# Turning M5's result back on VectorE instead of TensorE in the last unit of a fused attention and expert kernel

## The chip, the cores and the metric

The kernel runs on one core of one Trainium2 chip. A core has five engines that run beside each other, each with an instruction queue of its own: TensorE (PE, with PEld for its weight loads), VectorE (DVE), ScalarE (ACT), GpSimd (POOL) and SyncE (SP), which here does nothing but issue transfers. Transfers between the core's memory and HBM are issued from SP's queue and, now and then, from ScalarE's; the core's 16 DMA engines move the data. The metric is the device time of one execution in microseconds, lower being better.

## The reference

A block-wise attention with decay gives `x`, 3072 tokens by 512. Four experts follow, each two products with a ReLU between, and their results are summed with a weight per token:

```
def _moe_ref(x, domain_probs, w1, w2):
    p = domain_probs / (domain_probs.sum(-1, keepdims=True) + 1e-09)
    out = np.zeros((N, D), dtype=np.float32)
    for e in range(E):                      # E = 4, D = 512, F = 1024
        h = np.maximum(x @ w1[e], 0.0)
        out += p[:, e:e + 1] * (h @ w2[e])
    return out
```

Everything is float32. The change touches only the way in which one part of `out`, for the last 1024 tokens, is written.

## The kernel before, in words

The tokens are worked in three groups of 1024; a unit is one group with one expert, twelve units in all. Each expert product is a Strassen-like product of seven parts, M1 to M7, over 2 x 2 blocks, so that TensorE does seven block products instead of eight. In the later units the second product is nested: each of the seven is again made of seven inner ones (`nested_product`; `inner` issues one of them, with the matmuls of line 1550 and the VectorE adds into `sums`, recorded at line 117). `SEQ3`, line 1271, is the order of the outer products in a nested unit: M1, M3, M5, M7, M6, M2, M4. `INNER`, line 328, is the order of the inner ones: M1, M7, M6, M4, M5, M2, M3. Two banks of TensorE's output memory take turns in an outer product; `READ` says which inner product goes on in a bank that VectorE has read before.

`sums[m]` holds the result of outer product m for all the experts of the last group, features on the partitions and tokens along the free axis: four pieces of 128 x 256, piece 2*dd + t for feature half dd and token half t. After the last unit's products the seven are added into each other (`to_join`, `joined`, `bring`, `add`), and M2, M3, M4 and M5 then hold the four quadrants of `out` (`RESULT`). M5's quadrant is token half 1 and feature half 1. Since `out` has tokens along its rows, each quadrant has to be turned. Two helpers do that:

- `give(m, t, tags, dds)` (line 1369): 128 x 128 transposes by TensorE into a bank (line 1377; four of them for both feature halves), one ScalarE copy of the bank to a tile `y` (line 1381), and one transfer of 256 rows with 1 KB each, issued by SP (`send`, line 114).
- `give_across(m, dd, t)` (line 1390): one VectorE transpose in blocks of 32 x 32 (line 1398, 128 x 256), and four transfers (line 1402) of 256 pieces of 128 bytes each, 32 KB in all; the second of the four is issued by ScalarE, the other three by SP.

The last outer product, M4, is taken to its end on TensorE: `turn_end` (line 1440) turns its first feature half into a bank and `turned_product` (line 1450) adds the last two inner products there; ScalarE copies (line 1454) and SP stores. M4's other feature half goes through `give` with one `dd`.

The engines' queues hold their instructions in the order in which the program issues them, and an engine does not pass a waiting instruction. The order in the last unit is written out by hand. For outer product i the list `order` has eight slots; slot x holds some of the inner products. After slot x > 0 the loop takes the next entry of `after_last[SEQ3[i]]` and turns what it names. With M2 as the outer product these are M3's pieces, by `give_across`; with M4, before the change, M5's two token halves after slots 1 and 2 and M2's two after slots 3 and 4, by `give`. For M4, slots 1, 3, 5 and 7 hold inner products 0 and 1; 2 and 3; 4, with the first half of M4's ending; and the rest with the second half. So M5's first `give` stands on each queue after inner products 0 and 1.

Each transfer signals its landing on one of eight semaphores, which are dealt out in turn over both issuing queues. A transfer that is dealt a semaphore again waits, on the queue that issues it, until the earlier one on it has landed.

Of the kernel before, what the change touches and what calls it, by code (L numbers as in the profile page):

```python
# [21 lines left out]
def kernel(  # L22
# [66 lines left out]
    def bank(tag, name):  # L89
        return ps.tile([P, W], FP32, name=name, tag=tag)  # L90
# [567 lines left out]
    def fits():  # L658
        return filled[0] - now[0] < 0.6
# [611 lines left out]
    SEQ3 = ("M1", "M3", "M5", "M7", "M6", "M2", "M4")  # L1271
# [61 lines left out]
    def joined(m=None, k=None):  # L1333

        while m in apart:
            take(aside, True)
        while joins and (m is None or any(m == x and k in (None, y) for to, _ in joins for x, y in to)):
            joins.pop(0)[1]()
            if m is None:
                return  # L1340
# [28 lines left out]
    def give(m, t, tags, dds=(0, 1)):  # L1369

        joined(m)
        i, j = RESULT[m]
        p, o = bank(tags[t % len(tags)], "yp"), small("y")
        w = len(dds) * P
        for x, dd in enumerate(dds):
            for s in range(2):
                nc.tensor.transpose(  # L1377
                    out=p[:, s * w + x * P:s * w + (x + 1) * P], in_=sums[m][:, 2 * dd + t, s * P:(s + 1) * P],
                    identity=ident[:],
                )  # L1380
        nc.scalar.copy(out=o[:, 0:2 * w], in_=p[:, 0:2 * w])
        r, d = token(LAST, j, 2 * t), i * DH + dds[0] * P
        send(
            out=out[r:r + 256, d:d + w].rearrange("(s p) d -> p s d", p=P),
            in_=o[:, 0:2 * w].rearrange("p (s d) -> p s d", s=2),
        )
# [45 lines left out]
    END = FINAL, SEQ3[-1]  # L1432
# [391 lines left out]
    def pause_till(i, x):  # L1824
# [14 lines left out]
    fill3 = [(u, m, k) for u in range(NEST, len(units)) for m in SEQ3 for k in range(4)]  # L1839
    after_last = {  # L1840
        "M2": ((), (), (("M3", 0, 0), ("M3", 0, 1)), (), (("M3", 1, 0), ("M3", 1, 1))),
        "M4": ((("M5", 0),), (("M5", 1),), (("M2", 0),), (("M2", 1),)),
    }
    attention()
    PACE = 1.0, 1.0, 1.0
# [4 lines left out]
    for at, (g, e) in enumerate(units):  # L1850
        if at == 0:
            chores.extend(prepare_w2(2) + prepare_w1(3) + prepare_w2(3))
            chores.extend(prepare_w2_ops(2, False) + prepare_w1(0))
            for x in (3, 0):
                chores.extend(prepare_w2_ops(x, True))
        ahead = units[at + 1] if at + 1 < len(units) else None
        nested, nests = at >= NEST, ahead and at + 1 >= NEST
        if at == NEST:
            until(("w1", 0, "M4"))
            chores.extend(prepare_w2_ops(1, True))  # L1860
            spare.append(True)
        if at == NEST - 1:
            packed.append(True)
        blocks, banks = {}, {}
        for i in range(7):
            if fill2:
                feed2(*fill2.pop(0))
            if not nested:
                later_operands(g, e, SEQ2[i])
            if nested or (nests and i == 6):  # L1870
                for _ in range(4 if not nested else 2 if ahead else 16 if i == 0 else 4 if i > 1 else 0):
                    if fill3:
                        feed3(*fill3.pop(0))
            if nests and i == 2:
                nc.scalar.dma_start(
                    out=gate_bc, in_=gate_rows[ahead[0] - 1, :, ahead[1]].partition_broadcast(P),
                )
            if nested:
                pair = (at * 7 + i) % 2 if ahead else i % 3
                idle[:] = [(("q11", "q12"), ("q01", "q02"))[pair % 2], False]  # L1880
                b = nested_product(at, SEQ3[i], (("q01", "q02"), ("q11", "q12"), ("g1", "g3"))[pair])
                if i < 6 and (at, SEQ3[i + 1]) != PLAIN:
                    inner_sums(at, SEQ3[i + 1])
            else:
                b = second_product(g, e, SEQ2[i], banks)
            if nests and i == 6:
                inner_sums(at + 1, SEQ3[0], nested)
                if at + 1 == EARLY[0]:
                    inner_sums(*EARLY, True)
            a = []  # L1890
            if ahead:
                a = first_product(*ahead, SEQ[i], blocks, ("g1", "g3"))
            if nested and (at, SEQ3[i]) == END:
                b[6:6] = [lambda: (give("M4", 1, ("s0", "s1"), (1,)), turn_end(1, "q11"))]
                b[5:5] = [lambda: (give("M4", 0, ("s0", "s1"), (1,)), turn_end(0, "q12"))]
            if not ahead:
                order = [[], b[0:2], [], b[2:4], [], b[4:6], [], b[6:]]
            elif nested:
                order = [b[0:2], a[0:2], b[2:4], a[2:4], b[4:5], a[4:6], b[5:8], a[6:]]
            else:  # L1900
                order = [b[0:1], a[0:2], b[1:2], a[2:4], b[2:3], a[4:6], b[3:5], a[6:]]
            turned_back = list(after_last.get(SEQ3[i], ())) if nested and not ahead else []
            if at == i == 0:
                for m in SEQ[1:]:
                    own_x_apart(m, g, 0)
            resting[0] = at == NEST - 1 and i >= 5 or at == NEST and i == 0 or at == NEST - 2 and i == 5
            for x, part in enumerate(order):
                for f in part:
                    if f:
                        f()  # L1910
                now[0] += 1
                put = False
                if at == 0:
                    idle[:] = [("s0", "s1"), i < 3]
                    put = put_back()
                    take(own_sums)
                if nested and ahead:
                    idle[1] = x in ((1, 4) if i < 5 or at > NEST + 1 else (4,)) and (at - 2 * E + 1, i, x) not in held_at
                    put = put_back()
                added = first_steps.pop((at - 2 * E + 1, i, x), None)  # L1920
                if added:
                    added()
                all_added(now[0])
                if joins and not background:
                    joined()
                elif added and x > 2 or put:
                    pass
                elif (ahead or x % 2 == 0 and x + i) and not (nests and i == 6 and x == 7):
                    if nested or nests:
                        if lately:  # L1930
                            take(lately)
                        else:
                            rest()
                        if at == 2 * E and i in (2, 3) and fits():
                            rest()
                    else:
                        took = False
                        for of in (lately, background, own_sums):
                            if of and (not took or fits() or of is background and len(of) > 4):
                                take(of)  # L1940
                                if of is lately and i == 0:
                                    take(of)
                                took = True
                if nested or nests:
                    take(aside)
                    if own_sums and (nested or fits()):
                        take(own_sums)
                if ending and fits():
                    end_first()
                if nested and ahead and x in (1, 3) and fill3:  # L1950
                    feed3(*fill3.pop(0))
                if turned_back and x > 0:
                    for y in turned_back.pop(0):
                        if SEQ3[i] == END[1]:
                            give(*y[:2], ("s0", "s1"), *y[2:])
                        else:
                            give_across(*y)
                if fill and at * 7 + i >= 6 and x in ((0, 1) if at * 7 + i < 13 else (1, 3, 5) if at * 7 + i == 13 else FEED[nested]):
                    feed(*fill.pop(0))
                while steps and (at * 7 + i) * 8 + x == steps[0][0]:  # L1960
                    steps.pop(0)[1]()
                if at == 0 or x % 2 or at == 1 and x == 4:
                    trickle(1, nc.scalar if x % 2 else None)
                for h in range(1, NG):
                    if x == 3 and 0 <= at * 7 + i - FILL[h] < 7:
                        x_fill(h, SEQ[at * 7 + i - FILL[h]])
                pump(PACE[g])
# [30 lines left out]
```

## Time and profile before

| | us |
|---|---|
| runs shown (three) | 1141.19, 1141.27, 1144.36; median 1141.27 |
| the profiled execution | 1142.07 |
| its span, first to last instruction | 1140.3 |
| last product of the second-last outer product (M2) starts | 1121.21, takes 7.07 |
| first matmul of M4, the last one | 1128.12 |
| ScalarE's copies of M5's two token halves | from 1130.48, together 1.07 |
| ScalarE's last copy | 1137.05, takes 0.37 |
| last store issued | 1137.44 |

The profile is one execution, recorded instruction by instruction. The page gives busy times by engine; a timeline merges neighbouring equal instructions into a row (start, duration, engine, line, operation, result and operands, count, and the idle time before it with what ended it). Rows of SPq and ACTq are transfers as they are issued, not as they move. The chain of waits goes back from the last instruction, at each step to what released it. The granted TensorE clock is 0.999 over the whole span.

### The profile page before, as it was taken

Reading aid. Unit: us, or ns where it says so; the run is one execution under the profiler, and the core shown is the slowest. Engines: PE = TensorE matmul, PEld = TensorE weight load, DVE = VectorE, ACT = ScalarE, POOL = GpSimd, SP = SyncE. Lnnn points to the kernel's source line nnn. Section 1 sums busy time; section 2 is a strip of 40 time slices with the busy share of each in tenths; the row PEclk is TensorE's granted clock in tenths of the full one; section 3 lists DMA queues with packets and bytes.
Section 4 is the critical chain, followed back from the end, with each engine's and each line's share of the span. In section 5 each row is a group of like instructions: output and inputs, shape, how many; then the busy total and the mean of one; then the engine's idle time right before and its main releaser. Section 6 shows DMA issues by size and latency. Waiting matters only on the chain.

```text
span 1140.3 us, 22080 instructions
## 1 busy us (share of the span) xinstructions
PE 1130.5 (99%) x7983; PEld 988.2 (87%) x7983; DVE 769.0 (67%) x1474; ACT 380.3 (33%) x768; POOL 761.0 (67%) x730
## 2 busy tenths in 40 slices
PE   8999999999999999999999999999999999999998
PEld 7888888888888888888888888888888888888887
DVE  4576776587577658737655566878767576776785
ACT  3325123212312321232343442444354452342332
POOL 2838147644843786447687997994996873873885
PEclk9999999999999999999999999999999999999999
DMA  9795889999899989769557858886577757657552
GB/s 204 180 287 166 212 222 279 291 270 335 262 292 320 316 291 282 222 222 314 177 177 261 283 180 281 290 272 204 180 264 244 218 162 207 194 160 211 171 194 74
DMA packets 326828, 267.12 MB, mean 234 GB/s; under 512 B 153216, under 2 KB 270144, under 8 KB 326720
## 3 DMA queue, kind: packets, MB, share of 16 engines
q1 hardware_dynamic: 289472, 258.14, 73.1%
q10 hardware_dynamic: 37216, 7.57, 3.5%
q8 instruction: 64, 1.05, 0.4%
q14 instruction: 44, 0.36, 0.1%
q0 software_dynamic: 32, 0.00, 0.0%
HBM read 197.97 MB, written 73.96 MB: 238 GB/s over the span
## 4 chain that ended last, share of the span: by engine, by line
PE 98%; DVE 1%; issue 0%; DMA 0%; ACT 0%; DVEq 0%; POOLq 0%; ACTq 0%
PE pg L1174 41%; PE pq L1550 25%; PE q L1233 21%; PE pM L1692 2%; PE pc L1692 2%; PE op L824 1%; PE sp L761 1%; PE op L842 1%; PE sp L768 1%; PE pM L1417 1%; PE pg L1550 1%; PE qp L727 1%; PE kp L727 0%; DMA decay<-in_lam_dram 0%; PE yp L1377 0%
## 5 line engine op out<-in xcount | busy, mean ns | idle before, releaser
L1174 PE MATMUL pg<-xs,ws_in 128*128 128x256 f32 x1960 | 470.1, 380 | 0.0
L1174 PEld LDWEIGHTS pg<-xs,ws_in 128*128 128x128 f32 x1960 | 371.1, 190 | 52.8 <-DVE m L117 2.4
L117 DVE TENSOR_TENSOR m<-pg,m 128x512 f32<-128x512 f32 x374 | 255.4, 685 | 92.4 <-PE pg L1174 82.5
L1233 PE MATMUL q<-w2t,m 128*128 128x256 f32 x1120 | 265.6, 380 | 0.0
L1233 PEld LDWEIGHTS q<-w2t,m 128*128 128x128 f32 x1120 | 211.7, 190 | 29.3 <-issue 0.3
L117 DVE TENSOR_TENSOR sums<-pq,sums 128x256 f32<-128x256 f32 x272 | 112.9, 420 | 90.6 <-PE pq L1550 76.9
L1550 PE MATMUL pq<-acc,w2t 128*128 128x256 f32 x688 | 169.2, 379 | 0.0
L117 POOL TENSOR_TENSOR m<-m,decay 128x512 f32<-128x512 f32 x91 | 114.5, 1270 | 78.7 <-ACT m L1191 52.1
L1550 PEld LDWEIGHTS pq<-acc,w2t 128*128 128x128 f32 x688 | 130.6, 190 | 17.9
L1191 ACT ACTIVATE m<-m 128x512 f32<-128x512 f32 x99 | 62.4, 630 | 192.5 <-DVE m L117 190.6
L1251 DVE SCALAR_TENSOR_TENSOR acc<-q,gate,acc 128x256 f32<-128x256 f32 x108 | 52.0, 482 | 79.1 <-PE q L1233 78.6
L117 DVE TENSOR_TENSOR m<-m,m 128x512 f32<-128x512 f32 x108 | 92.9, 861 | 6.5 <-ACT m L1157 6.5
L1187 ACT COPY m<-pg 128x512 f32<-128x512 f32 x88 | 51.5, 585 | 122.0 <-PE pg L1174 108.7
L1151 ACT COPY pg<-m 128x512 f32<-128x512 f32 x77 | 45.4, 590 | 113.0 <-DVE m L117 103.3
L117 POOL TENSOR_TENSOR acc<-hT,hT 128x512 f32<-128x512 f32 x56 | 70.3, 1272 | 15.0 <-PE pq L1550 9.9
L117 POOL TENSOR_TENSOR acc<-hT,acc 128x512 f32<-128x512 f32 x56 | 71.2, 1272 | 6.4 <-PE pq L1550 2.7
L1550 PE MATMUL pq<-hT,w2t 128*128 128x256 f32 x288 | 70.0, 379 | 0.0
L117 POOL TENSOR_TENSOR w2o<-w2b 128x512 f32<-128x512 f32 x26 | 33.9, 1325 | 45.8 <-DMA w2b<-in_moe_w_dram 39.3
L1550 PEld LDWEIGHTS pq<-hT,w2t 128*128 128x128 f32 x288 | 54.7, 190 | 7.4
L1155 ACT COPY m<-pg 128x512 f32<-128x512 f32 x44 | 25.7, 585 | 89.6 <-PE pg L1174 84.8
L1550 PE MATMUL pq<-m,w2t 128*128 128x256 f32 x228 | 55.4, 379 | 0.0
L1005 ACT COPY hp<-m 128x512 f32<-128x512 f32 x84 | 48.5, 589 | 15.6 <-DVE hT L117 14.1
(157 smaller groups left out, 1419.5 us busy)
## 6 DMA issues: line engine op xcount, KB each, us to landing
ws_in<-w_ops SPq DMA_DIRECT2D x40, 512.0 KB, 5.1
w2t<-w_ops SPq DMA_DIRECT2D x72, 256.0 KB, 3.2
ws_in<-w_ops SPq DMA_DIRECT2D x60, 256.0 KB, 3.5
ws_in<-w_ops SPq DMA_DIRECT2D x40, 384.0 KB, 4.0
w2b<-in_moe_w_dram SPq DMA_DIRECT2D x56, 256.0 KB, 5.0
w_ops<-ops SPq DMA_DIRECT2D x28, 512.0 KB, 5.5
w_ops<-ops SPq DMA_DIRECT2D x54, 256.0 KB, 4.3
w2t<-w_ops SPq DMA_DIRECT2D x100, 128.0 KB, 2.8
```

What stands on the lines that cost most here:

```text
L117: eng.tensor_tensor(out=o, in0=a, in1=b, op=op)
L727: nc.tensor.transpose(out=x[:, ac * C:(ac + 1) * C], in_=y[:, ac].rearrange("p r d -> p (r d)"), identity=ident[:],)
L1005: nc.scalar.copy(out=there[x][:], in_=blk[at][:])
L1151: nc.scalar.copy(out=banks[tags[1]][:], in_=new["11"][:])
L1155: nc.scalar.copy(out=o[:], in_=p[:])
L1174: nc.tensor.matmul(out=p[:, j * 256:(j + 1) * 256], lhsT=ws[i][:, j * P:(j + 1) * P], rhs=xs[i], start=(fresh and j == 0), stop=True, skip ...
L1187: nc.scalar.copy(out=new[at][:], in_=p[:])
L1191: nc.scalar.activation(out=new[at][:], in_=new[at][:], func=AF.Relu)
L1233: nc.tensor.matmul(out=p[:, s * DH:(s + 1) * DH], lhsT=h[A_OF[m]][:, c * 256 + s * P:c * 256 + (s + 1) * P], rhs=fed2[g, e, m][uu][:, c], ...
L1251: nc.vector.scalar_tensor_tensor(out=o, in0=x, scalar=w, in1=o, op0=ALU.mult, op1=ALU.add)
L1550: nc.tensor.matmul(out=p[:, 0:256], lhsT=fed3[e, m, i][:, c * P:(c + 1) * P], rhs=b[B_OF[i]][:, c * 256:(c + 1) * 256], start=(fresh and c ...
L1692: nc.tensor.matmul(out=p[:, s * 256:(s + 1) * 256], lhsT=a[c][:, f:f + P], rhs=b[:, c, j * 256:(j + 1) * 256], start=(s == 0 and c == 0 an ...
```

## The change

In the last outer product, M4, the order after the slots is rewritten. M5's result is now named in pieces (feature half, token half) and goes through `give_across`; M2's halves keep `give` and their place after slots 3 and 4. M5's first feature half (both token halves) comes after slot 2 and its second after slot 5, behind the first half of M4's ending.

```diff
     after_last = {
         "M2": ((), (), (("M3", 0, 0), ("M3", 0, 1)), (), (("M3", 1, 0), ("M3", 1, 1))),
-        "M4": ((("M5", 0),), (("M5", 1),), (("M2", 0),), (("M2", 1),)),
+        "M4": ((), (("M5", 0, 0), ("M5", 0, 1)), (("M2", 0),), (("M2", 1),), (("M5", 1, 0), ("M5", 1, 1))),
     }
...
                 if turned_back and x > 0:
                     for y in turned_back.pop(0):
-                        if SEQ3[i] == END[1]:
-                            give(*y[:2], ("s0", "s1"), *y[2:])
+                        if len(y) == 2:
+                            give(*y, ("s0", "s1"))
                         else:
                             give_across(*y)
```

On the engines this takes out eight TensorE transposes (128 x 128), two ScalarE copies (128 x 512) and two stores of 256 KB on SP. It adds four VectorE transposes (128 x 256), twelve stores of 32 KB on SP and four on ScalarE. The order of the changed program's last instructions is:

```
VectorE: ... first two adds of M4, 2 transposes of M5, two adds, two adds, 2 transposes of M5
ScalarE: 4 stores of M3, 2 stores of M5, 2 copies of M2, 1 copy of M4, 2 stores of M5, 3 copies of M4
SP:      12 stores of M3, 6 of M5, 2 of M2, 1 of M4, 6 of M5, 3 of M4
```

By the turn in which the eight semaphores are dealt, SP's first store of M2 shares one with ScalarE's third store of M5, and SP's first store of M4 with ScalarE's fourth; both of those on ScalarE come before in the dealing.

## The prediction

> **What bounds the kernel now.** I read the page's busy times first, then the chain that ended last over the final 20 us, then the timeline of that stretch queue by queue, then the waits of SP's queue, and last the landing times there. The first lines are the page's; the rest are, in order, the chain (share by line, and its last pieces), the timeline, the waits of SP's queue, the transfers of line 1402 and the issues with their landing times.
>
> ```profile
> span 1140.3 us, 22080 instructions
> PE 1130.5 (99%) x7983; PEld 988.2 (87%) x7983; DVE 769.0 (67%) x1474; ACT 380.3 (33%) x768; POOL 761.0 (67%) x730
> ...
> by line: PE pM L1417 32.9%; PE pq L1550 27.8%; PE yp L1377 10.4%; PE yp L1450 8.6%; PE yp L1440 2.1%; ACT y L1454 1.8%; issue 0.1%
> ...
> 1130.01 0.87 PE yp L1377 x8
> ...
> 1137.05 0.37 ACT y L1454
> ...
> 1126.14 0.77 DVE L1398 STREAM_TRANSPOSE y<-sums 128x256 f32<-128x256 f32 x2
> 1126.60 5.82 SPq L1402 DMA_DIRECT2D out_dram<-y  x12
> 1126.61 2.72 ACTq L1402 DMA_DIRECT2D out_dram<-y  x4
> ...
> 1128.00 0.75 DVE L1398 STREAM_TRANSPOSE y<-sums 128x256 f32<-128x256 f32 x2
> ...
> 1129.85 0.74 DVE L117 TENSOR_TENSOR sums<-pq,sums 128x256 f32<-128x256 f32 x2
> ...
> 1132.52 5.30 SPq L114 DMA_DIRECT2D out_dram<-y  x8
> ...
> 1134.39 0.76 DVE L117 TENSOR_TENSOR sums<-pq,sums 128x256 f32<-128x256 f32 x2 [1.31 <-PE pq L1550]
> ...
> SPq L114 <- ACT y L1381: 1.5, 3, 1.0
> ...
> L1402 SPq DMA_DIRECT2D out_dram<-y x12: 349/448/461, 1126.6 to 1132.0; - x12
> ...
> out_dram<-y SPq DMA_DIRECT2D x4, 128.0 KB, 2.2
> out_dram<-y SPq DMA_DIRECT2D x12, 32.0 KB, 1.7
> out_dram<-y ACTq DMA_DIRECT2D x4, 32.0 KB, 1.9
> ```
>
> TensorE is busy for 99% of the span and the chain runs along it to its last product; then come one copy by ScalarE (1137.05) and the last store, issued at 1137.44. From that issue to the end are 1140.3 - 1137.44 = 2.86 us. So 1 us less TensorE is worth 1 us only as long as the last store waits for ScalarE's copy. The SPq rows show how near another limit is: the 12 block stores of M3 go out without a gap from 1126.60 to 1132.42 though their last transpose ended at 1128.75, one per (1132.52 - 1126.60) / 12 = 0.49 us. SP's own issuing sets that pace. The next 8 stores take 5.30 us; 8 at 0.49 would be 3.9. So only about 1.4 us of slack is left on SP before the end, where it waits for ScalarE (1.5 us, three times).
>
> **The change, part by part.** *TensorE.* Eight transposes go, 0.87 us of chain at 1130.01. Not all of it is gained: the next matmuls write the bank that the first of the two adds at 1129.85 reads, and that add ends at 1130.26. They started at 1130.72 and may start between 1130.3 and (with a weight load of 0.2 us behind the wait) 1130.55: a gain of 0.17 to 0.42 us, taken as 0.3. Two ScalarE copies (1.07 us) go with them.
>
> *VectorE.* Four transposes are added, in pairs of 0.76 us like the rows at 1126.14 and 1128.00. The first pair stands behind the adds that end at 1130.59 and runs to 1131.35; the next add has its product at 1131.79 - 0.3 = 1131.5, so the pair costs nothing, and at most 0.15 us if TensorE gains 0.42. The second pair is VectorE's last work. It follows the adds at 1134.39, which end at 1135.15, now at 1134.85.
>
> *The queues.* Two 256 KB stores on SP go; 12 stores of 32 KB come on SP, 4 on ScalarE. SP's order of the changed program is: 12 stores of M3 as before, 6 of M5, 2 of M2, 1 of M4, 6 of M5, 3 of M4. ScalarE's is: 2 stores of M5, three copies, 2 stores of M5, three copies. Price of one on SP: 0.49 us, from the twelve. The bare instruction is 0.35 to 0.46 us there and the larger stores of line 114 stand 0.5 apart too (1132.52, 1133.02), so size is not what sets it. From 1126.60 to the end SP had 20 stores and now has 30: 10 x 0.49 = 4.9 us more.
>
> *The wait that is added.* Each transfer signals one of eight semaphores in turn, and the next user of a semaphore waits until the one before has landed. In the changed program M2's first store (SP) takes the semaphore of M5's third ScalarE store, though it stands ahead of it in the work; so it waits until that one has landed, and that one waits for VectorE's second pair. M4's first store likewise waits for the fourth, which lands at 1135.75 + 1.9 = 1137.65, before SP comes to it (1138.2). Behind M2's first store on SP stand all 11 others. The ScalarE store: in M3 it was issued 0.47 us after its transpose began (1126.14, 1126.61). The second pair begins at 1134.8, so issue 1135.27; landing takes 1.9 us (ACTq row): 1137.17. SP is done with M5's first six at 1132.52 + 6 x 0.49 = 1135.5 and stands still for 1.7 us. On ScalarE the copy for M4 behind these two stores goes from 1135.77 to about 1136.2; its store is far back in SP's queue, so that costs nothing.
>
> *The sum.* M2's first store 1137.2; eleven more, 11 x 0.49 = 5.4: the last is issued at 1142.6. From issue to end 2.86 us, and 0.25 more, because that last store landed in the least of its kind (1.8 us; median of the four 128 KB ones 2.2), and now three go out half a us apart: 1145.7. That is 5.4 us over 1140.3. The profiled execution took 1142.07 us, 1.8 outside its span, so 1147.5 for that one; the runs shown have a median of 1141.27, 0.8 below it, so 1146.7 us beside them, 0.47% slower.
>
> *Bounds.* ScalarE store: issue 1135.15 to 1135.45, landing 1.6 to 2.0, so M2's first store 1136.8 to 1137.5. Eleven issues at 0.45 to 0.55 (the steps between 1127.00, 1127.50, 1128.05, 1128.55 and 1129.00 among the twelve): 4.95 to 6.05. Tail 2.86 to 3.5. Span 1144.6 to 1147.0: beside the median 1145.6 to 1148.0.
>
> The Trainium skill, "DMA: Bandwidth & Descriptors", section "Issuing engines are not separate DMA queues", says that the time a sequencer needs to start a transfer is usually small beside the transfer itself. The twelve rows disagree for stores this small (0.45 us of instruction each, 5.82 in a row, against 1.7 to land); by the page's rule SP would not be the bound and the time would be the second rival's, 1141.0 us, where the rows give 1146.7.
>
> **The rivals.** *SP does not wait for ScalarE's store* (the two queues' order works out otherwise, or the landing comes early). For it: in the profile before no SP store waits for a landing in mid-queue. Against: the wait is written in the program. Then M2's first store goes at 1135.5, the last at 1140.9; with 3.0 behind it 1143.9: +3.6, 1144.9 us.
>
> *Faster: TensorE still sets the end.* One mechanism: SP's 30 stores drain as fast as their data come, so the last store again follows ScalarE's last copy. It decides once an issue costs under (1137.1 - 1135.5) / 11 = 0.15 us with the semaphore wait gone, and the gain is the 0.3 us of TensorE, at most 0.87: 1140.4 to 1141.0 us. For it: TensorE is 99% busy and does lose the transposes. Against: twelve stores with their data ready at 0.49 us each.
>
> *The DMA engines are the bound, not SP.* From 1132.5 to 1137.9 they were busy for 88% of the time in the windows view, and stores then took up to 2.9 us to land. If the landings of ScalarE's store and of the last one both stretched by 1 us, +7.4: 1148.7 us. Against: with 16 block stores on both queues (1126.6 to 1132.5) the share was 52%.
>
> **How the numbers follow.** A measurement of this kernel can tell 0.3% (3.4 us) from no change. Forecast 0.80; no wait on ScalarE's store 0.10; DMA-bound 0.07; faster 0.03. The forecast's own range lies wholly beyond +3.4. The first rival lies on that edge (+3.6): 0.06 of its 0.10 counts as slower and 0.04 as no change. So slower 0.93, no change 0.04, faster 0.03. The range reaches from just under the first rival to just over the forecast's upper bound: 1144.5 to 1148.3 us.
>
> **What would show it.** Right: SPq rows without a gap from 1126.60 to about 1135.5, a gap of 1 to 2 us ahead of the first store of line 114, ended by the landing of a store of ScalarE's, then 12 at 0.49 us; TensorE done near 1136.7 and ScalarE's last copy near 1137.1, over 5 us ahead of the last issue. Wrong: no such gap (first rival); a last store that still follows the last copy at once (second); landings near 3 us among the last stores (third). The TensorE step is wrong if the first matmuls after M4's opening pair start near 1129.85 or still at 1130.7.

## The result, and the profile after

The changed kernel is slower by 0.6%: a ratio of 1.0061 with a 95% interval of 1.0041 to 1.0081, that is 7.0 us (4.7 to 9.3) on the 1143.29 us that is the median of seven runs of the kernel before. The changed kernel's own median is 1149.49 us (seven runs, 1146.83 to 1154.32), 6.2 us above the other median. A second series of twelve gave 1149.77 us and 1.0052 (1.0032 to 1.0072). The forecast was 1146.7 us in a range of 1144.5 to 1148.3: the direction is right, and the ratio it implies, 1.0047, lies in both intervals, but the time lies 1.2 us above the range.

The profiled execution of the changed kernel is one of the long ones, 1154.32 us. Its page's first lines:

```profile
span 1152.5 us, 22084 instructions
...
PE 1131.4 (98%) x7975; PEld 987.2 (86%) x7975; DVE 769.3 (67%) x1478; ACT 379.0 (33%) x766; POOL 763.9 (66%) x730
```

The granted TensorE clock is 0.996 here against 0.999 before, but that is not the cause: in the windows view it is 0.99 up to 300 us in both profiles, 1.00 from there to 1145 us in this one, and falls to 0.58 only after that, behind TensorE's last product, which ends at 1143.46.

The chain of waits over its last 25 us, in shares by line. Over the last 20 us before the change TensorE's five lines made 32.9 + 27.8 + 10.4 + 8.6 + 2.1 = 81.8% of it and VectorE none; now VectorE's adds and transposes hold 24%, and ScalarE's stores of line 1402 are in it:

```profile
by line: DVE sums L117 16.0%; PE pq L1550 15.7%; PE pM L1417 13.9%; DVE y L1398 8.2%; issue 4.3%; PE yp L1377 3.5%; ACTq L1402 1.8%; ACT y L1454 1.5%; DVEq L1993 1.3%; ACTq L1993 1.1%; ACT y L1381 1.1%; DVEq L117 0.1%; ACTq L1454 0.1%
```

The timeline of the end, by queue: SP's transfers, ScalarE with its own, VectorE, TensorE (start, duration, engine, line, operation, count, and the idle time before with what ended it):

```profile
1133.30 8.92 SPq L1402 DMA_DIRECT2D out_dram<-y  x18
1143.84 1.44 SPq L114 DMA_DIRECT2D out_dram<-y  x3
1145.38 2.97 SPq L1402 DMA_DIRECT2D out_dram<-y  x6
1148.45 1.44 SPq L114 DMA_DIRECT2D out_dram<-y  x3
...
1141.98 0.82 ACTq L1402 DMA_DIRECT2D out_dram<-y  x2
...
1143.71 0.39 ACT L1454 COPY y<-yp 128x256 f32<-128x256 f32 x1
...
1137.21 0.75 DVE L1398 STREAM_TRANSPOSE y<-sums 128x256 f32<-128x256 f32 x2
...
1141.51 0.76 DVE L1398 STREAM_TRANSPOSE y<-sums 128x256 f32<-128x256 f32 x2
...
1137.09 0.45 PE L1550 MATMUL pq<-acc,w2s 128*128 128x256 f32 x1 [0.39 <-DVE sums L117]
```

SP's four rows are the whole story of the end. Eighteen block stores go out without a pause until 1142.22, then nothing for 1.6 us, then twelve more at half a us each. ScalarE's last copy starts at 1143.71, and the last store is issued only at 1149.45 (the last row's end, 1149.89, less one issue of 0.44). In the profile before, these two were 0.39 us apart. What ended the pause is in the waits of SP's queue over the last 25 us (who waited for what: us in total, times, longest):

```profile
SPq L114 <- DMA out_dram<-y: 1.6, 1, 1.6
```

A store waited 1.6 us for the landing of another store. ScalarE's third store of M5, issued at 1141.98, lands 1.80 us later, at 1143.78, and SP goes on at 1143.84; the trace has both stores on the same semaphore. Experiments below take this landing away.

To set executions beside each other I take the start of line 1417's first matmul as zero; from there on the two programs differ. Before, it starts at 1121.21 and the span ends at 1140.3; after, at 1127.91 and 1152.5. The rows of these matmuls, before and after (first and last start at the end):

```profile
L1417 PE MATMUL pM<-m,w2s x32: 379/379/379, 1121.2 to 1127.9; 128*128 128x256 f32 x32
```

```profile
L1417 PE MATMUL pM<-m,w2s x32: 379/379/379, 1127.9 to 1134.6; 128*128 128x256 f32 x32
```

This stretch is called the tail below:

| us from the first matmul of line 1417 | before | after | forecast |
|---|---|---|---|
| first matmul behind M4's opening two inner products starts | 9.51 | 9.18 | 9.2 |
| ScalarE's third store of M5 issued | | 14.07 | 14.06 |
| M2's first store issued | 12.5 | 15.93 | 16.0 |
| last store issued | 16.23 | 21.54 | 21.4 |
| end of the span | 19.1 | 24.6 | 24.5 |

The tail became 5.5 us longer. The profiled execution is 12.2 us longer: the other 6.7 us arose ahead of line 1417, in work that is the same instructions in both kernels.

### The profile page after: what moved, and what is told of

Same layout as the page of the kernel before. It is cut to its first block, busy times and chain, and to the rows that moved or that the text cites. A ratio compares the mean times of both kernels' runs of the same rounds, so it can differ in the third digit from the quotient of the medians.

```text
span 1152.5 us, 22084 instructions
## 1 busy us (share of the span) xinstructions
PE 1131.4 (98%) x7975; PEld 987.2 (86%) x7975; DVE 769.3 (67%) x1478; ACT 379.0 (33%) x766; POOL 763.9 (66%) x730
## 4 chain that ended last, share of the span: by engine, by line
PE 93%; SPq 2%; DVE 2%; DMA 1%; issue 1%; ACTq 0%; ACT 0%; DVEq 0%
PE pg L1174 40%; PE pq L1550 24%; PE q L1233 21%; PE pc L1692 2%; PE pM L1692 2%; SPq L114 1%; SPq L178 1%; PE op L824 1%; PE sp L761 1%; PE op L842 1%; PE sp L768 1%; DMA ws_in<-w_ops 1%; DVE m L117 1%; PE pg L1550 1%; DMA kn<-in_k_dram 0%
## 5 line engine op out<-in xcount | busy, mean ns | idle before, releaser
L117 DVE TENSOR_TENSOR m<-m,m 128x512 f32<-128x512 f32 x108 | 89.6, 830 | 7.4 <-ACT m L1157 7.4
L1005 ACT COPY hp<-m 128x512 f32<-128x512 f32 x84 | 48.5, 589 | 15.6 <-DVE hT L117 14.1
```

Source lines behind the costliest of these rows:

```text
L117: eng.tensor_tensor(out=o, in0=a, in1=b, op=op)
L1005: nc.scalar.copy(out=there[x][:], in_=blk[at][:])
```

## The experiments

Four of the kernels below ran once each (M5's stores all on SP, ScalarE's two late stores left out, ScalarE's four alone, spread without GpSimd); of these only the tail is read.

**Both kernels once more.** No edit. This asks whether those 6.7 us belong to the change.

> The changed kernel as it is, profiled a second time. I measure the tail, from the first matmul of line 1417 to the span's end: 19.1 us before, 24.6 us after. Theory (the tail is the whole effect; the 4.8 us that TensorE waited for ws_in at 247 us in the first profile is chance): tail 24.6 within 0.3 us, no such wait at 247 us, the span about 1146, the time 5 to 6 us (0.5%) over the kernel before. Rival (the change disturbs the transfers of the early units as well): the same wait of 4 to 5 us again near 247 us, the time 8 us or more over.

> The kernel before, profiled a second time, to see how far two executions of one program differ ahead of the tail. Theory (chance): tail 19.1 within 0.3 us, the ratio 1.000 within 0.002, and the time up to the first matmul of line 1417 (1121.2 us in the first profile) different by some us. Rival (the kernel before is steady and only the changed one is not): that time within 0.5 us of 1121.2.

The row of line 1417's matmuls again. First the kernel before, again, with a span of 1144.7 us:

```profile
L1417 PE MATMUL pM<-m,w2s x32: 379/379/379, 1125.6 to 1132.3; 128*128 128x256 f32 x32
```

and the changed kernel, again, with a span of 1144.5 us:

```profile
L1417 PE MATMUL pM<-m,w2s x32: 379/379/379, 1119.9 to 1126.6; 128*128 128x256 f32 x32
```

The tails are 19.1 and 24.6 us again, to 0.02 us the same as in the first profiles. The time ahead of them is not steady in either kernel: 1121.2 and 1125.6 us before, 1127.9 and 1119.9 after. This time the changed kernel's span is the shorter of the two. The kernel before against itself gave 1.0002 (0.998 to 1.0023). Its 35 runs beside these experiments reach from 1141.36 to 1150.12 us with a median of 1144.45. So the 6.7 us are scatter. The largest single piece of it is seen in the waits of TensorE between 240 and 260 us, of the changed kernel's first profile and of the second one of the kernel before:

```profile
PE pg L1174 <- DMA ws_in<-w_ops: 4.6, 1, 4.6
```

```profile
PE pg L1174 <- DMA ws_in<-w_ops: 2.9, 1, 2.9
```

A weight load lands late near 246 us. In eight of the twelve profiles of this study TensorE stood there for such a load for over 2 us, in a ninth for 3.0 us, put down to VectorE, and in the first of the kernel before and the second of the changed one not at all.

**SP without the wait for ScalarE's store, by way of GpSimd.**

```diff
-            by = nc.scalar if a == 1 else nc.sync
+            by = nc.gpsimd if a == 1 and m == "M5" else nc.scalar if a == 1 else nc.sync
```

> The changed kernel with M5's four ScalarE stores issued by GpSimd, which has no work left there. SP's list of 30 stores stays the same, and none of them shares a semaphore with a late store any more. Theory (SP's pace, and a wait for ScalarE's store on top): no gap on SP's queue, 29 steps of 0.49 us from M3's first store, last issue at 5.4 + 14.3 = 19.7 us of the tail, tail 22.6 to 22.8, about 1.8 us less than after. Rival (the gap costs nothing, another limit lies at 24.6, the DMA engines say): tail 24.3 or more. If GpSimd is so slow that its own stores land last, its queue shows it.

Measured: tail 23.5 us (ratio 1.0044, 1.0027 to 1.0061). The pause is gone, but the gain is 1.1 us and not 1.8. SP's timeline shows where the rest went, the row of a single issue:

```profile
1140.54 1.03 SPq L1402 DMA_DIRECT2D out_dram<-y  x1
```

One issue took 1.03 us and the next 0.62, where the others take about 0.45. Neither side was quite right: the pause cost time, and part of what was saved went into issues that took longer.

**SP without the wait, by leaving stores out.**

```diff
+            if (m, dd, a) == ("M5", 1, 1):
+                continue
             by = nc.scalar if a == 1 else nc.sync
```

> The changed kernel without M5's last two ScalarE stores, so 64 KB of M5's quarter are not written. SP keeps its 30 stores in the same order; by the order in which semaphores are now dealt none of them shares one with a late store. Theory (30 issues, and on top of them the wait for ScalarE's store): no gap, last issue at 5.4 + 29 x 0.495 = 19.7 to 19.8 us of the tail, tail 22.6 to 22.8, so the wait is worth 1.8 to 2.0 of the 5.5 us and SP's ten more issues the rest. Rival (the gap only moves; something else holds SP before M2's first store): a gap of over 1 us stays, tail 24 or more.

SP's timeline, in which block stores are line 1404 here:

```profile
1131.36 8.88 SPq L1404 DMA_DIRECT2D out_dram<-y  x18
1140.33 1.94 SPq L114 DMA_DIRECT2D out_dram<-y  x3
1142.37 2.95 SPq L1404 DMA_DIRECT2D out_dram<-y  x6
1145.41 1.44 SPq L114 DMA_DIRECT2D out_dram<-y  x3
```

The pause of 1.6 us between the first two rows has shrunk to an ordinary step, so the landing of ScalarE's store is what it waited for. The second row's three issues take 1.94 us where they took 1.44 after: the third of them, at 1141.33, lasted 0.94. The tail is 23.5 us, below the rival's 24 and above the 22.8 I had expected. So the wait is worth 1.1 us as things stand, and the other 4.4 us remain with thirty issues and no wait.

**Issues in place of the wait.**

```diff
-            by = nc.scalar if a == 1 else nc.sync
+            by = nc.scalar if a == 1 and m != "M5" else nc.sync
```

> The changed kernel with M5's four ScalarE stores moved to SP, so that no store of SP's waits for one of ScalarE's; SP then has 34. Theory (gap and issue time add up on one queue): no gap, 33 steps of 0.49 to 0.50 us, last issue at 21.6 to 21.9, tail 24.5 to 24.8: as after, four issues taking the place of the gap. Rival (the wait is the cost, issuing is cheap): tail 22.9 or less.

```profile
1127.92 9.76 SPq L1402 DMA_DIRECT2D out_dram<-y  x20
1137.78 1.45 SPq L114 DMA_DIRECT2D out_dram<-y  x3
1139.33 3.95 SPq L1402 DMA_DIRECT2D out_dram<-y  x8
1143.38 1.44 SPq L114 DMA_DIRECT2D out_dram<-y  x3
```

SP's timeline: 34 stores, no pause from 1127.92 to 1144.82, 16.9 us / 34 = 0.50 us each. The tail is 24.9 us (expected 24.5 to 24.8). No store waits for a landing, and the end comes 0.3 us later than in the changed kernel: four issues cost more than the wait did.

**TensorE as before, M5's result in 16 stores.** This takes VectorE out of the change and keeps the number of stores.

```diff
+        if m == "M5":
+            for s in range(2):
+                for a in range(4):
+                    by = nc.scalar if a == 1 else nc.sync
+                    by.dma_start(
+                        out=out[r + s * P + a * 32:r + s * P + (a + 1) * 32, d:d + w],
+                        in_=o[a * 32:(a + 1) * 32, s * w:(s + 1) * w],
+                    )
+            return
         send(
```

> The kernel before, with TensorE turning M5 back as ever, but each of M5's two stores cut into 8, a row block of 32 x 256 each (32 pieces of 1 KB): 12 on SP, 4 on ScalarE. VectorE does nothing new. Theory (it is the number of stores on SP that costs, whoever turns and however many pieces a store has): 30 stores at 0.49 us, last issue at 5.4 + 14.2 = 19.6 us of the tail, tail 22.2 to 22.8. Rival (the price goes by the pieces; these stores have 32 where the block stores have 256, so some 0.06 us each): the last issue follows ScalarE's last copy as before, tail 19.1 to 19.6.

SP's timeline (line 1411 is M3's block stores here, 1387 M5's row blocks):

```profile
1129.11 6.87 SPq L1411 DMA_DIRECT2D out_dram<-y  x12
1136.07 5.76 SPq L1387 DMA_DIRECT2D out_dram<-y  x12
1141.93 3.06 SPq L114 DMA_DIRECT2D out_dram<-y  x6
```

and the wait for a landing in SP's queue:

```profile
SPq L1411 <- DMA out_dram<-y: 1.5, 3, 1.1
```

From its first store of M5 to its first of M2 SP takes (1141.93 - 1136.07) / 12 = 0.49 us per store of 32 pieces, as it does for one of 256 pieces. Both are 32 KB; but SP's stores of 256 KB stand 0.49 us apart too (1143.84 and 1144.33 in the changed kernel). So neither pieces nor size set the price: it goes by the store. The tail is 24.2 us against 22.2 to 22.8 expected; the ratio is 1.0060 (1.0041 to 1.0078), like that of the change, with TensorE and VectorE as before. Most of the excess is again a wait between the queues: M3's stores stood 1.5 us for landings here, 1.1 us of it for ScalarE's first store of M5. My expectation had left out that ScalarE's stores take their turns among the semaphores here as well.

**M5's stores left out.**

```diff
-        for a in range(4):
+        for a in range(4 if m != "M5" else 0):
```

> The changed kernel without M5's 16 stores, so that M5's quarter of the last 1024 tokens is not written; the transposes on VectorE stay. SP then has 18 stores where it had 20 before. Theory (stores are the whole cost, TensorE gains 0.25 us): the end follows ScalarE's last copy again, tail 18.8 within 0.2 us, the time the same as before. Rival (the transposes hold up VectorE and with it TensorE): tail over 19.3 us.

Tail 19.0 us, ratio 0.9999 (0.998 to 1.0018). The four transposes on VectorE hold up nothing, and TensorE ends 0.25 us earlier than before, as it does after the change. Of this 0.11 us reach the end. So with stores that cost nothing the change would have been worth a tenth of a us.

**ScalarE's four stores alone.**

```diff
+            if m == "M5" and a != 1:
+                continue
             by = nc.scalar if a == 1 else nc.sync
```

> The changed kernel with M5's four ScalarE stores alone, its twelve on SP left out, so three quarters of M5's quarter are not written. SP has 18 stores, none of which shares a semaphore with a late one of ScalarE's. Theory: ScalarE's four stores cost nothing of their own; the end follows ScalarE's last copy (15.8 in after), tail 18.9 to 19.3. Rival (four stores ahead of the copies on ScalarE delay them and TensorE): last copy over 16.2, tail over 19.5.

The tail is 19.7 us, 0.7 more than with no store of M5 at all, and the theory's "nothing of their own" falls. ScalarE's timeline (line 1454 is 1456 here):

```profile
1136.92 0.84 ACTq L1404 DMA_DIRECT2D out_dram<-y  x2
1138.15 0.37 ACT L1456 COPY y<-yp 128x256 f32<-128x256 f32 x1 [1.78 <-PE yp L1377]
```

and the longest wait of SP's stores of line 114:

```profile
SPq L114 <- ACT y L1381: 3.1, 3, 2.0
```

M4's second copy stands behind the two stores, which wait for VectorE's last transposes, and starts at 1138.15, 15.3 us into the tail, where it started at 14.3 with no stores there. SP, which has time here, waits for it: its store of this copy goes at 1138.55, just behind the copy's end at 1138.52. (The row puts the wait down to line 1381, whose next copy starts before this one has ended.) TensorE isn't held up (its last product ends at 15.6 us in both). In the changed kernel SP was the later one, and this cost was covered.

**The stores spread.** The first edit below, with GpSimd; a second version sends M5's first half to ScalarE (every second store) and its second half to SP.

```diff
-        "M4": ((), (("M5", 0, 0), ("M5", 0, 1)), (("M2", 0),), (("M2", 1),), (("M5", 1, 0), ("M5", 1, 1))),
+        "M4": ((), (("M5", 0, 0), ("M5", 0, 1)), (("M5", 1, 0), ("M5", 1, 1), ("M2", 0)), (("M2", 1),)),
...
-            by = nc.scalar if a == 1 else nc.sync
+            by = (nc.scalar if m == "M3" else nc.gpsimd) if a % 2 else nc.sync
```

In the second version the last line reads:

```diff
+            by = nc.scalar if a % 2 and (m == "M3" or dd == 0) else nc.sync
```

> The changed kernel with the block stores spread: every second one of M3's on ScalarE (8 and 8), every second one of M5's on GpSimd (8 and 8), and M5's second half turned after slot 3 and not after slot 5. SP has 22 stores, 20 before the change. Theory: the last issue follows ScalarE's last copy again, and what TensorE saves comes out at the end: tail 18.8 to 19.1 (before 19.07), too little for the time to show. Rival (GpSimd's stores slow SP's issues or land late, as they did by 0.9 us in the run with four of them): tail 19.5 to 21.

> As the spread version, but without GpSimd: M5's first half goes every second store to ScalarE, its second half wholly to SP. SP has 26 stores, no semaphore shared with a late one. Theory: 25 steps of 0.49 us from 5.4, last issue at 17.6 to 17.8, tail 20.4 to 20.7. Rival (ScalarE's stores hold up its copies and TensorE with them): ScalarE's last copy later than 15.9 of the tail.

With GpSimd the tail is 21.0 us (ratio 1.0053, 1.0039 to 1.0067), without it 22.3 us; both expectations were too low, and the first one's rival held. In the version with GpSimd SP issues its last store 1.4 us after ScalarE's last copy began, so SP is nearly out of the way, but the stores land late; the transfers of its last stretch (KB each, median us to landing):

```profile
out_dram<-y SPq DMA_DIRECT2D x2, 256.0 KB, 3.4
out_dram<-y SPq DMA_DIRECT2D x4, 128.0 KB, 3.5
```

In the changed kernel these two rows read 2.5 and 1.9 us. Six large stores in a row do not explain it: in the version without GpSimd and in the one with M5's 16 stores from TensorE six go out in a row as well, and the rows read 2.4 and 2.3, and 2.4 and 2.4. In the version without GpSimd three of SP's steps were some 0.45 us too long, which my expectation had not counted: twice SP stood for VectorE's transposes, and once the issue itself lasted 0.91 us. Neither version reaches the kernel before, and since no more than 0.1 us was to be had, I looked no further for one.

## Why the prediction was right and wrong

- *TensorE gains 0.17 to 0.42 us, not 0.87.* Right. The matmuls that follow waited 0.39 us for VectorE's add (the last line of the timeline above) and started 0.33 us earlier than before.
- *The transposes on VectorE cost nothing.* Right, shown without the stores: ratio 0.9999.
- *0.49 us per store on SP, ten stores more.* Right in place and in size: 18 stores took 8.92 us. That size doesn't set the price is shown by the stores of 256 KB, that the number of pieces doesn't by the stores of 32 pieces (0.49 us apart, both).
- *M2's first store waits for ScalarE's third store of M5.* Right: issue of that store, pause and resumption came within 0.1 us of the forecast. What it is worth was put too high: the first rival, without the wait, stood at +3.6 against +5.4, so at 1.8 us. The pause is 1.6 us, but taking the wait away gave back only 1.1, because some issues then lasted longer.
- *ScalarE's stores ahead of M4's copies cost nothing, since their stores are far back on SP.* Right in the changed kernel. The price without that cover was not given; it is 0.7 us.
- *The sum, 1145.7 - 1140.3 = 5.4 us.* The tail grew by 5.5.
- *1146.7 us, range 1144.5 to 1148.3.* Wrong. The step that failed is the last one of the sum, "the runs shown have a median of 1141.27, 0.8 below it, so 1146.7 us beside them", and with it the bounds, which hold nothing but the terms of the tail. Three runs were taken for the kernel's level. That level, mis-sized by 2 to 3 us, is 1143.29 by seven runs and 1144.45 by 35. Of the 2.8 us by which the time missed, 2.0 are this level; the other 0.8 is the distance of the medians, 6.2 instead of 5.4, which the interval of 4.7 to 9.3 us does not tell apart. With 5.4 us on the level of the 35 runs the forecast would have been 1149.9, and twelve runs of the changed kernel gave 1149.8; that it fits so closely is partly luck, given the scatter. A base that scatters by 9 us also needs a range that has this scatter in it. One of the three runs, at 1144.36, had shown it.

The three rivals: SP did wait; the faster one had SP's issue price wrong by the trace itself, and M5's 16 stores from TensorE, slower by as much with VectorE doing nothing new, exclude it; that the DMA engines were the bound is contradicted by median landings of 1.7 to 2.5 us in the changed kernel's tail.

The Trainium skill, "DMA: Bandwidth & Descriptors", section "Issuing engines are not separate DMA queues", takes the time to start a transfer as usually small beside the transfer; here one start, 0.48 to 0.50 us, is below a landing of 1.7 us, but thirty of them on one queue were the bound. The same section says that transfers issued from any engine run on the same DMA engines and interleave. The version with GpSimd fits this: with eight stores on its queue, SP's larger ones took 3.4 and 3.5 us to land, against 2.4 and 2.3 in the version without. That GpSimd's stores are the cause is not shown: without ScalarE's late stores, and without GpSimd, the 256 KB stores took 3.0 us as well.

## What to carry to other kernels

Count the issues on each queue before cutting a transfer into small ones: a queue that is within some 1.4 us of the end has no room for ten more at half a us, whatever the engine that they relieve. Where transfers on two queues share semaphores in turn, a late one on one queue can stop the other, so look up which of them share one. And before a forecast in absolute time, see how far the kernel's own runs lie apart; a difference of some us can be read from a stretch of the trace that repeats to 0.02 us even when whole executions differ by 9.

## What the runs showed that I had not expected

Some issues on SP lasted up to twice as long as the rest: 0.94 us without ScalarE's late stores, 1.03 with four stores on GpSimd, 0.89 and 0.98 in the spread version with GpSimd, 0.91 in the one without, against 0.32 to 0.47 for all others but three (0.62 to 0.67). Most stood among or right behind large stores, but the 0.91 stood among stores of 32 KB. And in the profile before four stores of 256 KB went out in a row with issues of 0.37 to 0.42 us, and in the changed kernel's tail none lasted so long either. What holds them is open; no run here isolates it. The DMA view gives a lead: in both spread versions and in the run without ScalarE's late stores a load of 8 KB of instructions starts within 0.15 us of a long issue (the page calls its queue q14 instruction). It is no more than a lead, since in the changed kernel such a load at 1143.78 stretched no issue, and the run with four stores on GpSimd has a long issue with none near.
